# Four of six chunks of a matmul as seven products in every second group, with four-bank evictions and sums by accumulating DMA

## The chip, the cores and the metric

The kernel runs on one core of a Trainium2 chip. Its time is the device time of one execution, in microseconds (us). Before the change it was 1006.78 us, the median of three runs (1006.6 to 1006.91). The profile is of one more execution, with a span of 1005.2 us.

## The reference, cut to what matters

A depthwise causal convolution along the sequence, with seven taps per head and softmax over the taps, then layer norm, then a two-layer block with a residual:

```python
# x: (8, 4224, 192) fp32; weight: (8 heads, 7 taps)
w = softmax(weight, axis=-1)
y[b, s, d] = sum_k w[d // 24, k] * x_pad[b, s + k, d]     # six zeros ahead of each sequence
xn = (y - mean(y)) / sqrt(var(y) + 1e-6) * g_ln           # over d
out = y + relu(xn @ w_ch1) @ w_ch2                        # 192 -> 768 -> 192
```

All is fp32. The weights of the two matmuls come as fp64 and are converted in the kernel; the mean and g_ln are folded into w1, and the division by the standard deviation is applied after the second matmul, as one scale per position (relu allows it).

## The kernel before

Each sequence of 4224 positions is laid out as 128 partitions by 33 rows. The rows are cut into 18 groups: four small ones for the first sequence, then 16 and 17 rows in turn for each of the other seven. While TensorE does group g, VectorE and ScalarE prepare y of group g + 1 and g + 2 (taps), and finish g - 1.

The first matmul ("up", tile ph) makes 768 hidden values in six chunks of 128. A transpose in 32x32 blocks puts 32 channels on partitions, so four matmuls of 32 rows, one for each quarter of the partitions, run side by side; each writes a PSUM bank of its own:

```python
    psum = ctx.enter_context(tc.tile_pool(name="ps", bufs=8, space=PSUM))
    # ... up(g), cut
        for f in range(NF):                               # 6 chunks
            fs = slice(f * P, f * P + P)
            for js in blocks(g):                          # 1 block for 16 rows, 2 for 17
                w = (js.stop - js.start) * C
                ph = [psum.tile([P, 512], F32, tag="ps", ...) for q in range(NQ)]
                for c in range(NC):                       # 6 slices of 32 channels
                    for q in range(NQ):                   # 4 quarters of the partitions
                        rows = slice(C * q, C * q + C)
                        nc.tensor.matmul(
                            ph[q][:, 0:w], w1[rows, c, fs], t[rows, js, c, :],
                            start=(c == 0), stop=(c == NC - 1),
                        )
                for q in range(NQ):
                    # ... dst and src, cut
                    nc.scalar.activation(dst, src, AF.Relu)
            # ... f = 1 to 4: scale and add_to_out of group g - 1, a quarter at a time
```

The second matmul ("down_fast", tile pd) is already done by seven products in place of eight (a Strassen-Winograd scheme: sums of quarters of the hidden values and of w2, seven half-size products, sums of the results). The hidden values are summed in place on VectorE:

```python
    def down_fast(g):
        # ... cs, part, six banks
        def product(bank, left, right, to, first):
            for c in range(CH):
                dst = banks[2 * c + bank]
                # ... matmuls over f and q into dst
                nc.scalar.copy(to[:, c], dst[:, 0:w].rearrange("p (j t) -> p j t", t=T))
        # ... todo: the first and second tap of group g + 2, head by head, on ScalarE
        product(0, a[:, 0, 0], b[0], c11, True)
        some_taps(3)
        product(1, a[:, 1, 0], w2sums[:, 2], c22, True)
        some_taps(3)
        product(1, a[:, 1, 1], w2sums[:, 3], part[:, 1], False)
        some_taps(3)
        product(1, a[:, 0, 1], b[2], part[:, 0], True)
        some_taps(3)
        half_sum(g, (1, 1), (1, 1), (1, 0), ALU.subtract)     # three adds of 1024 each
        half_sum(g, (0, 0), (1, 1), (0, 0), ALU.add)
        half_sum(g, (0, 1), (0, 1), (1, 1), ALU.subtract)
        nc.vector.tensor_tensor(c11, c11, part[:, 0], op=ALU.add)
        product(0, a[:, 1, 1], w2sums[:, 1], c21, False)
        some_taps(2)
        product(0, a[:, 0, 0], w2sums[:, 0], part[:, 2], False)
        some_taps(2)
        product(0, a[:, 0, 1], b[3], c12, False)
```

The second tap of y is added by a DMA that accumulates, from a buffer tb; the other five taps run on VectorE (conv). The loop over groups, for those with seven products:

```python
        up(g)
        conv(g + 1, 2, 5)
        half_sum(g, (1, 0), (0, 0), (1, 0), ALU.subtract)     # the "lower sum"
        conv(g + 1, 5, K)
        transpose(g + 1)
        store_y(g + 1)
        parts = down_fast(g)
        moments(g + 1)                                        # mean and variance per position
        if g % 2 == 0:
            root(g)
        for half in range(last, 2):
            finish_fast(g, half, *parts)                      # add, transpose back
```

Of the kernel before, what the change touches and what calls it, by code (L numbers as in the profile page):

```python
# [16 lines left out]
def kernel(  # L17
# [8 lines left out]
):  # L26

# [17 lines left out]
    nc = tc.nc  # L45
# [33 lines left out]
    T = C // 2  # L79
    CH = NC // 2  # L80
# [11 lines left out]
    spool = ctx.enter_context(tc.tile_pool(name="stat", bufs=3))  # L92
# [4 lines left out]
    psum = ctx.enter_context(tc.tile_pool(name="ps", bufs=8, space=PSUM))  # L97
# [137 lines left out]
    w2sums = consts.tile([P, 4, FC, D // 2], F32, name="w2sums")  # L235
    copy, less, mean = carve(P, F32), carve(P, F32), carve(F, F32)
# [37 lines left out]
    def conv_on_pe(h):  # L274
        n = groups[0][2]
        cs = slice(h * GRP, h * GRP + GRP)
        pc = psum.tile([P, 512], F32, tag="ps", name=f"pc{h}")[:, 0 : n * GRP]
        for k in range(K):
            nc.tensor.matmul(  # L279
                pc, diag[:, h - PE_HEADS[0], k, :], xg[0][:, k : k + n, cs],  # L280
                start=(k == 0), stop=(k == K - 1),
            )
        nc.scalar.copy(y[0][:, 0:n, cs], pc.rearrange("p (j d) -> p j d", d=GRP))

    def centre_w1():
        pm = [psum.tile([P, 512], F32, tag="ps", name=f"pm{r}")[:, 0:FH] for r in range(2)]
        for r in range(2):
            nc.tensor.matmul(pm[r], share[0], w1f[:, r, :], start=True, stop=False)  # L288
        conv_on_pe(PE_HEADS[0])
        for r in range(2):  # L290
            nc.tensor.matmul(pm[r], share[1 + r], w1f[:, 2, :], start=False, stop=True)  # L291
            nc.scalar.copy(mean[:, FH * r : FH * r + FH], pm[r])
        conv_on_pe(PE_HEADS[1])
        first_tap(1, heads=(0, 2))

        for s, parts in (
            (0, [(q, 0) for q in range(NQ)]),
            (2, [(NQ, 0), (NQ + 1, 0), (NQ, 1), (NQ + 1, 1)]),
            (1, [(q, 1) for q in range(NQ)]),
        ):  # L300
            pw = [psum.tile([P, 512], F32, tag="ps", name=f"pw{s}_{q}") for q in range(NQ)]
            for q in range(NQ):
                rows = slice(C * q, C * q + C)
                nc.tensor.matmul(  # L304
                    pw[q][:, 0:FH], copy[rows], w1f[rows, s, :], start=True, stop=False
                )
            for q, (c, r) in enumerate(parts):
                rows = slice(C * q, C * q + C)
                nc.tensor.matmul(  # L309
                    pw[q][:, 0:FH], less[rows], mean[rows, FH * r : FH * r + FH],  # L310
                    start=False, stop=True,
                )
            for q, (c, r) in enumerate(parts):
                nc.scalar.copy(w1[:, c, FH * r : FH * r + FH], pw[q][:, 0:FH])
            if s == 0:
                conv_on_pe(PE_HEADS[2])
                first_tap(1, heads=(2, 4))

    def keep_warm(times):

        idle = psum.tile([P, 512], F32, tag="ps", name="idle")
        for _ in range(times):
            nc.tensor.matmul(idle[:, 0:P], less, copy, start=True, stop=True)
# [66 lines left out]
    def moments(g):  # L390

        n = groups[g][2]
        if g % 2:
            sums[g] = sums[g - 1][:, groups[g - 1][2] :]
        else:
            sums[g] = spool.tile([P, 2 * J, nc.vector.BN_STATS_DIM], F32, tag="st", name=f"st{g}")
        for j in range(n):
            nc.vector.bn_stats(out=sums[g][:, j, :], in_=y[g][:, j, :])  # L398
# [53 lines left out]
    def up(g):  # L452


        n = groups[g][2]
        scaled = {0: (), 1: (), 2: (0, 1)}.get(g, (g - 1,))
        t = yt[g]
# [4 lines left out]
        if fast[g]:  # L462
            halves = room[:, 0:cut].rearrange(
                "p (h e f q j t) -> p h e f q j t", h=2, e=2, f=FC, q=NQ, t=T
# [5 lines left out]
        ht[g] = halves, rest  # L470
        for f in range(NF):
            fs = slice(f * P, f * P + P)
            for js in blocks(g):
                w = (js.stop - js.start) * C
                ph = [
                    psum.tile([P, 512], F32, tag="ps", name=f"ph{g}_{f}_{js.start}_{q}")
                    for q in range(NQ)
                ]
                for c in range(NC):
                    for q in range(NQ):  # L480
                        rows = slice(C * q, C * q + C)
                        nc.tensor.matmul(  # L482
                            ph[q][:, 0:w], w1[rows, c, fs], t[rows, js, c, :],
                            start=(c == 0), stop=(c == NC - 1),
                        )
                for q in range(NQ):
                    src = ph[q][:, 0:w]
                    if js.stop <= fast[g]:
                        dst = halves[:, :, f // FC, f % FC, q, js].rearrange("p h j t -> p j h t")
                        src = src.rearrange("p (j h t) -> p j h t", h=2, t=T)  # L490
                    else:
                        dst = rest[:, f, q, js.start - fast[g] : js.stop - fast[g]]
                        src = src.rearrange("p (j t) -> p j t", t=C)
                    nc.scalar.activation(dst, src, AF.Relu)  # L494
            if 1 <= f <= 4:
                for s in scaled:
                    m = groups[s][2]
                    scale(s, m * (f - 1) // 4, m * f // 4)
                    if f % 2 == 0:
                        add_to_out(s, m * (f - 2) // 4, m * f // 4)  # L500

    po = {}

    def down(g):
# [8 lines left out]
        for c, js in order:  # L513
            w = (js.stop - js.start) * C
            bank = psum.tile([P, 512], F32, tag="ps", name=f"po{g}_{c}_{js.start}")
# [8 lines left out]

    def w2_sums():
        (b11, b12), (b21, b22) = (
            (w2[:, e * FC : e * FC + FC, 0 : D // 2], w2[:, e * FC : e * FC + FC, D // 2 : D])
            for e in range(2)  # L530
        )

        for dst, a, b in ((0, b12, b11), (1, b22, 0), (2, b22, b12), (3, b21, 1)):
            a, b = (w2sums[:, v] if isinstance(v, int) else v for v in (a, b))
            nc.vector.tensor_tensor(w2sums[:, dst], a, b, op=ALU.subtract)

    def half_sum(g, dst, left, right, op):
        a = ht[g][0]
        for f in range(FC):
# [3 lines left out]

    def down_fast(g):
        n = fast[g]
        w = n * T
        a = ht[g][0]
        cs = cpool.tile([P, NC, NFAST * C], F32, tag="cs", name=f"cs{g}")[:, :, 0 : n * C]
        cs = cs.rearrange("p c (j h t) -> p c j h t", h=2, t=T)
        part = cpool.tile([P, 3, CH, NFAST * T], F32, tag="part", name=f"part{g}")[:, :, :, 0:w]  # L550
        part = part.rearrange("p v c (j t) -> p v c j t", t=T)
        banks = [
            psum.tile([P, 512], F32, tag="ps", name=f"pd{g}_{c}_{i}")
            for c in range(CH) for i in range(2)
        ]

        def product(bank, left, right, to, first):
            for c in range(CH):
                dst = banks[2 * c + bank]
                for f in range(FC):  # L560
# [6 lines left out]
                nc.scalar.copy(  # L567
                    to[:, c], dst[:, 0:w].rearrange("p (j t) -> p j t", t=T)
                )

        b = [w2[:, e * FC : e * FC + FC, d * (D // 2) : (d + 1) * (D // 2)]
             for e in range(2) for d in range(2)]
        c11, c21 = cs[:, 0:CH, :, 0], cs[:, 0:CH, :, 1]
        c12, c22 = cs[:, CH:NC, :, 0], cs[:, CH:NC, :, 1]
# [8 lines left out]
        some_taps(3)  # L583
        product(1, a[:, 1, 0], w2sums[:, 2], c22, True)
        some_taps(3)
        product(1, a[:, 1, 1], w2sums[:, 3], part[:, 1], False)
        some_taps(3)
        product(1, a[:, 0, 1], b[2], part[:, 0], True)
        some_taps(3)
        half_sum(g, (1, 1), (1, 1), (1, 0), ALU.subtract)  # L590
        half_sum(g, (0, 0), (1, 1), (0, 0), ALU.add)
        half_sum(g, (0, 1), (0, 1), (1, 1), ALU.subtract)
        nc.vector.tensor_tensor(c11, c11, part[:, 0], op=ALU.add)
        product(0, a[:, 1, 1], w2sums[:, 1], c21, False)
        if g + 1 == NG:
            finish_fast(g, 0, cs, part)
        some_taps(2)
        product(0, a[:, 0, 0], w2sums[:, 0], part[:, 2], False)
# [3 lines left out]
        return cs, part  # L602

    def finish_fast(g, half, cs, part):
        n = fast[g]
        ot = ots[g] if half else out_tile(g)
        fresh = cs[:, CH * half : CH * half + CH, :, 1]
        nc.vector.tensor_tensor(fresh, fresh, part[:, 1 + half], op=ALU.add)  # L608
        for c in range(CH * half, CH * half + CH):
            nc.vector.transpose(  # L610
                ot[:, 0:n, C * c : C * c + C], cs[:, c].rearrange("p j h t -> p j (h t)")
            )

    def park(g):

        n = groups[g][2]
        room = 3 * CH * NFAST * T if g == 0 else NC * NFAST * C
        parked = cpool.tile([P, room], F32, tag="cs" if g else "part", name=f"parked{g}")
# [77 lines left out]
    for g in range(NG):  # L696
        if g + 2 < NG and g not in (3, 4):
            load_x(g + 2)
        up(g)
        last = g + 1 == NG  # L700
        if g == 0:
            first_tap(1, False, heads=(4, H))
        if not fast[g]:
# [14 lines left out]
            if g == 1:  # L718
                finish(0)
                root(0)  # L720
                w2_sums()
# [7 lines left out]
        if not last:  # L729
            conv(g + 1, 2, 5)  # L730
        half_sum(g, (1, 0), (0, 0), (1, 0), ALU.subtract)
        if not last:
            conv(g + 1, 5, K)
            transpose(g + 1)
            if g != 3 and g + 2 < NG:
                store_y(g + 1)
# [6 lines left out]
        if not last:  # L743

            moments(g + 1)
            if g % 2 == 0:
                root(g)
        for half in range(last, 2):
            finish_fast(g, half, *parts)
        if last:  # L750
# [33 lines left out]
```

## Time and profile before

| engine | busy us | share of the span |
|---|---|---|
| PE (TensorE matmul) | 993.9 | 99% |
| PEld (TensorE weight load) | 660.8 | 66% |
| DVE (VectorE) | 844.1 | 84% |
| ACT (ScalarE) | 559.9 | 56% |
| POOL (GpSimd) | 65.7 | 7% |

Of the span, the first matmul has 518.3 us of TensorE, the second 418.9 us (236.9 + 182.0) in groups with seven products and 51.4 us in the others. The clock granted to TensorE is full throughout. A line of the profile names an engine, a line of the kernel, an operation, and the tiles it writes and reads; what follows in square brackets is the idle time ahead of it and what ended it. In the pieces of the chain the columns are start, length, engine, tile and line, and the number of instructions.

### The profile page before, as it was taken

Reading aid. Unit: us, or ns where it says so; the run is one execution under the profiler, and the core shown is the slowest. Engines: PE = TensorE matmul, PEld = TensorE weight load, DVE = VectorE, ACT = ScalarE, POOL = GpSimd, SP = SyncE. Lnnn points to the kernel's source line nnn. Section 1 sums busy time; section 2 is a strip of 40 time slices with the busy share of each in tenths; the row PEclk is TensorE's granted clock in tenths of the full one; section 3 lists DMA queues with packets and bytes.
Section 4 is the critical chain, followed back from the end, with each engine's and each line's share of the span. In section 5 each row is a group of like instructions: output and inputs, shape, how many; then the busy total and the mean of one; then the engine's idle time right before and its main releaser. Section 6 shows DMA issues by size and latency. Waiting matters only on the chain.

```text
span 1005.2 us, 35683 instructions
## 1 busy us (share of the span) xinstructions
PE 993.9 (99%) x16050; PEld 660.8 (66%) x16050; DVE 844.1 (84%) x1552; ACT 559.9 (56%) x1468; POOL 65.7 (7%) x92
## 2 busy tenths in 40 slices
PE   7999999999999999999999999999999999999997
PEld 6888675578545875468654686557854578545786
DVE  7999898898788978979689896889968799788607
ACT  6547464656556564665646566465654656554451
POOL 2001101000000000000000000000001000000000
PEclk9999999999999999999999999999999999999999
DMA  5343717634336363254634535364243734142031
GB/s 193 108 191 55 204 31 219 203 65 110 133 72 194 65 194 88 37 191 84 194 69 83 182 58 182 68 153 137 44 171 75 219 65 106 46 77 37 2 65 69
DMA packets 16102, 114.17 MB, mean 114 GB/s; under 512 B 2127, under 2 KB 2895, under 8 KB 11854
## 3 DMA queue, kind: packets, MB, share of 16 engines
q0 software_dynamic: 9504, 54.17, 27.8%
q1 hardware_dynamic: 6142, 57.73, 14.5%
q8 instruction: 125, 2.05, 0.9%
q14 instruction: 27, 0.22, 0.1%
q10 hardware_dynamic: 304, 0.00, 0.0%
HBM read 38.95 MB, written 50.23 MB: 89 GB/s over the span
## 4 chain that ended last, share of the span: by engine, by line
PE 98%; DVE 1%; DMA 0%; ACT 0%; issue 0%; ACTq 0%
PE ph L482 51%; PE pd L562 40%; PE po L518 5%; PE pc L279 1%; DMA taps<-in_weight_dram 0%; DVE ht L540 0%; PE pw L304 0%; PE pw L309 0%; ACT room L272 0%; DVE y L647 0%; PE pm L288 0%; PE pm L291 0%; DVE room L205 0%; DVE room L197 0%; DVE room L194 0%; ACT room L181 0%
## 5 line engine op out<-in xcount | busy, mean ns | idle before, releaser
L482 PE MATMUL ph<-yt,w 32*128 32x256 f32 (+6 forms) x7200 | 518.3, 443 | 0.1
L482 PEld LDWEIGHTS ph<-yt,w 32*128 32x128 f32 x7200 | 364.3, 185 | 151.0 <-issue 116.3
L373 DVE SCALAR_TENSOR_TENSOR y<-xg,taps,y 128x408 f32<-128x408 f32 (+5 forms) x734 | 365.8, 575 | 33.4 <-issue 33.2
L494 ACT ACTIVATE ht<-ph 128x256 f32<-128x256 f32 (+6 forms) x600 | 222.6, 457 | 228.8 <-PE ph L482 228.1
L540 DVE TENSOR_TENSOR ht<-ht 128x1024 f32<-128x1024 f32 (+2 forms) x180 | 205.4, 1208 | 105.6 <-PE pd L562 74.8
L562 PE MATMUL pd<-ht,w2sums 128*32 128x256 f32 (+2 forms) x4320 | 236.9, 377 | 0.1
L562 PEld LDWEIGHTS pd<-ht,w2sums 128*32 128x32 f32 x4320 | 140.3, 110 | 91.2 <-DVE ht L540 0.5
L562 PE MATMUL pd<-ht,w 128*32 128x256 f32 (+2 forms) x3240 | 182.0, 378 | 0.0
L562 PEld LDWEIGHTS pd<-ht,w 128*32 128x32 f32 x3240 | 103.8, 110 | 73.9 <-issue 8.3
L567 ACT COPY cs<-pd 128x256 f32<-128x256 f32 (+2 forms) x180 | 66.5, 370 | 99.5 <-PE pd L562 99.5
L635 ACT ACTIVATE ot<-ot,r 128x192 f32<-128x192 f32 x247 | 93.1, 471 | 0.0
L567 ACT COPY part<-pd 128x256 f32<-128x256 f32 (+2 forms) x135 | 49.5, 368 | 73.6 <-PE pd L562 73.6
L346 ACT ACTIVATE y<-xg,taps 128x408 f32<-128x408 f32 (+5 forms) x137 | 71.7, 592 | 5.6 <-DVE st L398 5.1
L398 DVE BATCH_NORM_STATS2 st<-y 128x6 f32<-128x192 f32 x264 | 70.2, 342 | 0.0
L359 ACT ACTIVATE tb<-xg,taps 128x384 f32<-128x384 f32 (+1 forms) x112 | 63.4, 619 | 0.0
L639 POOL DMA_DIRECT2D out_dram<-ot x34 | 29.5, 883 | 459.9 <-ACT ot L635 269.3
L610 DVE STREAM_TRANSPOSE ot<-cs 128x512 f32<-128x512 f32 (+2 forms) x90 | 56.6, 679 | 2.5 <-DVE cs L608 0.5
L384 DVE STREAM_TRANSPOSE yt<-y 128x3072 f32<-128x3072 f32 (+5 forms) x19 | 56.2, 2957 | 2.1 <-PE ph L482 0.4
L518 PE MATMUL po<-ht,w 128*32 128x192 f32 (+3 forms) x1152 | 51.4, 339 | 0.0
L362 POOL DMA_DIRECT2D y<-tb x28 | 24.9, 1051 | 351.4 <-ACT cs L567 173.2
L518 PEld LDWEIGHTS po<-ht,w 128*32 128x32 f32 x1152 | 37.1, 110 | 13.7 <-issue 0.8
L608 DVE TENSOR_TENSOR cs<-cs,part 128x768 f32<-128x768 f32 (+2 forms) x30 | 27.7, 925 | 0.0
(79 smaller groups left out, 150.2 us busy)
## 6 DMA issues: line engine op xcount, KB each, us to landing
y<-tb POOLq DMA_DIRECT2D x21, 768.0 KB, 6.4
out_dram<-ot POOLq DMA_DIRECT2D x20, 768.0 KB, 6.8
xg<-in_x_dram SPq DMA_DIRECT2D x6, 2208.0 KB, 13.2
xg<-in_x_dram SPq DMA_DIRECT2D x6, 2112.0 KB, 13.0
out_dram<-y SPq DMA_DIRECT2D x6, 1632.0 KB, 7.8
out_dram<-y SPq DMA_DIRECT2D x6, 1536.0 KB, 8.3
y<-tb POOLq DMA_DIRECT2D x7, 864.0 KB, 10.6
out_dram<-ot POOLq DMA_DIRECT2D x6, 864.0 KB, 7.1
```

What stands on the lines that cost most here:

```text
L346: nc.scalar.mul(dst, src, tap)
L359: nc.scalar.mul(tb[g][:, 0:n, cs], xg[g][:, 1 : 1 + n, cs], taps[:, h, 1:2])
L373: nc.vector.scalar_tensor_tensor(out=y[g][:, 0:n, cs], in0=t[:, k : k + n, cs], scalar=taps[:, h, k : k + 1], in1=y[g][:, 0:n, cs], op0=AL ...
L398: nc.vector.bn_stats(out=sums[g][:, j, :], in_=y[g][:, j, :])
L482: nc.tensor.matmul(ph[q][:, 0:w], w1[rows, c, fs], t[rows, js, c, :], start=(c == 0), stop=(c == NC - 1),)
L494: nc.scalar.activation(dst, src, AF.Relu)
L518: nc.tensor.matmul(bank[C * q : C * q + C, 0:w], w2[:, f, C * c : C * c + C], t[:, f, q, js.start - fast[g] : js.stop - fast[g], :], start ...
L540: nc.vector.tensor_tensor(a[:, *dst, f], a[:, *left, f], a[:, *right, f], op=op)
L562: nc.tensor.matmul(dst[C * q : C * q + C, 0:w], right[:, f, C * c : C * c + C], left[:, f, q], start=(first and f == 0), stop=(f == FC - 1 ...
L567: nc.scalar.copy(to[:, c], dst[:, 0:w].rearrange("p (j t) -> p j t", t=T))
L610: nc.vector.transpose(ot[:, 0:n, C * c : C * c + C], cs[:, c].rearrange("p j h t -> p j (h t)"))
L635: nc.scalar.mul(ots[g][:, j, :], ots[g][:, j, :], rstd[g][:, j : j + 1])
```

## The change

In the six groups 6, 8, ..., 16 (16 rows each) the first matmul takes four of its six chunks in seven products. The rows of positions are halved (8 and 8), the channels are halved (3 and 3 slices), and the four chunks are two and two. Each product is then two chunks wide, 256 columns by 3 slices. The first and the last of the six chunks are done as before and stand ahead of and behind the products. The sums of y are made by VectorE in the buffer tb, the sums of w1 once. Three products accumulate in one set of four banks (the chain) and the running result is copied out between them; what must be added elsewhere is added by DMAs that accumulate in SBUF, and by VectorE for c21. Relu is applied in the last copy, or on SBUF after the sums.

For this PSUM is one tile of eight banks, given out singly or in sets of four; a set is copied out by one instruction in groups with an even number of rows. The order on VectorE and ScalarE is shifted around the products: the moments go ahead of the half sums in part, nine of the scalings go into the second matmul, and one copy in the second matmul (part 0) is left out, VectorE reading the bank instead. The purpose is fewer columns for TensorE, which is busy nearly all the time. The diff, cut:

```diff
+    MIXED = range(6, NG, 2)
+    PAIR = NF // 2 - 1
+    HJ = (J - 1) // 2
+    EARLY = 6
-    psum = ctx.enter_context(tc.tile_pool(name="ps", bufs=8, space=PSUM))
+    psum = ctx.enter_context(tc.tile_pool(name="ps", bufs=1, space=PSUM))
+    all_banks = psum.tile([P, 8, 512], F32, tag="ps", name="ps")
+    turn = [0]
+    def take_bank():
+        i = turn[0] % 8
+        turn[0] = i + 1
+        return all_banks[:, i]
+    def take_set():
+        i = (turn[0] + 3) // 4 * 4 % 8
+        turn[0] = i + 4
+        return all_banks[:, i : i + 4]
...
+    def sums_of_y(g):
+        room = bpool.tile([P, J * D], F32, tag="tb", name=f"ysums{g}")
...
+        nc.vector.tensor_tensor(s1, a21, a22, op=ALU.add)
+        nc.vector.tensor_tensor(s2, s1, a11, op=ALU.subtract)
+        nc.vector.tensor_tensor(s3, a21, a11, op=ALU.subtract)
+        nc.vector.tensor_tensor(s4, a12, s2, op=ALU.subtract)
+    def up_mixed(g):
...
+        banks = plain(PAIR)
+        scale(g - 1, 0, 4)
+        evict_up(g, PAIR, whole, banks)
+        conv(g + 1, 2, 6)
+        chain, other = take_set(), take_set()
+        rows_of_tiles(chain, a11, b11, True, False)
+        evict(chain, c11)
+        scale(g - 1, 4, 5)
+        rows_of_tiles(other, a12, b21)
+        evict(other, late[0])
+        add_by_dma(c11, late[0])
+        rows_of_tiles(chain, s2, w1sums[:, 1], False, False)
+        evict(chain, c21)
+        scale(g - 1, 5, 6)
+        rows_of_tiles(other, s3, w1sums[:, 2], True, False)
+        evict(other, c22)
+        scale(g - 1, 6, 7)
+        rows_of_tiles(chain, s1, w1sums[:, 0], False, False)
+        for i in range(PAIR):
+            one = slice(i, i + 1)
+            evict(chain, late[1 + i], i=one)
+            add_by_dma(c22[:, one], late[1 + i])
+        rows_of_tiles(other, a22, w1sums[:, 3], False)
+        evict(other, late[0])
+        scale(g - 1, 7, 8)
+        add_to_out(g - 1, 0, 8)
+        # c21 += late[0], two adds on VectorE (cut)
+        rows_of_tiles(chain, s4, b22, False)
+        evict(chain, c12, True)
+        nc.scalar.activation(c11, c11, AF.Relu)
+        lower_sum(g, (PAIR,))
+        lower_sum(g, range(PAIR))
+        conv(g + 1, 6, K)
+        banks = plain(PAIR + FC)
+        evict_up(g, PAIR + FC, whole, banks)
+        nc.scalar.activation(c22, c22, AF.Relu)
...
         product(0, a[:, 0, 0], b[0], c11, True)
-        some_taps(3)
+        if g in MIXED:
+            m = groups[g - 1][2]
+            scale(g - 1, 8, m)
+            add_to_out(g - 1, 8, m)
+            some_taps(1)
+        else:
+            some_taps(3)
...
-        product(1, a[:, 0, 1], b[2], part[:, 0], True)
+        product(1, a[:, 0, 1], b[2], None, True)
         some_taps(3)
-        half_sum(g, (1, 1), (1, 1), (1, 0), ALU.subtract)
+        if g in MIXED:
+            transpose(g + 1)
+            moments(g + 1, 0, EARLY)
+        elif g + 1 in MIXED:
+            moments(g + 1)
+            if g + 1 == MIXED[0]:
+                sums_of_quarters(w1sums, *quarters_of_w1())
+        half_sum(g, (1, 1), (1, 1), (1, 0), ALU.add)
...
-        nc.vector.tensor_tensor(c11, c11, part[:, 0], op=ALU.add)
+        # c11 += banks[2c + 1], read in PSUM by VectorE, three adds (cut)
...
         for half in range(last, 2):
             finish_fast(g, half, *parts)
+        if g + 1 in MIXED:
+            sums_of_y(g + 1)
+        if mixed:
+            moments(g + 1, EARLY)
+            root(g)
```

`plain(f)` takes a set and does one chunk as before; `evict` is one ScalarE instruction over the four banks.

## The prediction

> **What bounds the kernel now.** I read the chain that ended last first, for its engine shares, then its pieces in order of time.
>
> ```profile
> PE 98%; DVE 1%; DMA 0%; ACT 0%; issue 0%; ACTq 0%
> ```
>
> ```profile
> 77.80 15.75 PE ph L482 x288
> ...
> 394.97 31.11 PE ph L482 x288
> 426.08 27.33 PE pd L562 x504
> 453.42 33.21 PE ph L482 x576
> 486.63 29.01 PE pd L562 x504
> ```
>
> TensorE is the chain, with no gap between pieces. The line at 394.97 is the first matmul of group 8 (sixteen rows of positions, one of the six groups changed): 288 records, two per fp32 matmul, so 31.11/6 = 5.185 us per chunk of 48 records, 108.0 ns each at 512 columns. The line at 77.80 is group 2, whose matmuls are all 256 wide: 15.75/288 = 54.7 ns. So halving the width costs nearly nothing (2 x 54.7 against 108.0). The second matmul takes 27.33/7 = 3.90 us a product.
>
> Next the table by stage for that group and the following one (columns: busy time and instructions of each engine, clock, DMA share):
>
> ```profile
> 394.97:426.08 31.11, 31.11 (x293) 14.66 (x296) 27.97 (x47) 16.50 (x38) 1.74 (x2) 1.00 0.39 74
> 426.08:453.42 27.34, 27.34 (x509) 16.29 (x508) 22.01 (x37) 16.90 (x40) 1.78 (x2) 1.00 0.58 186
> ```
>
> VectorE is busy 28.0 + 22.0 of 58.4 us: 8.5 us spare, and the new design needs some of it. Where the spare lies is in VectorE's timeline:
>
> ```profile
> 397.62 2.00 DVE L610 STREAM_TRANSPOSE ot<-cs 128x544 f32<-128x544 f32 x3
> 402.65 13.39 DVE L373 SCALAR_TENSOR_TENSOR y<-xg,taps,y 128x408 f32<-128x408 f32 x24 [3.03 <-issue]
> 415.96 3.49 DVE L540 TENSOR_TENSOR ht<-ht 128x1024 f32<-128x1024 f32 x3
> 419.37 8.95 DVE L373 SCALAR_TENSOR_TENSOR y<-xg,taps,y 128x408 f32<-128x408 f32 x16
> 428.42 3.58 DVE L384 STREAM_TRANSPOSE yt<-y 128x3264 f32<-128x3264 f32 x1
> 437.15 10.30 DVE L540 TENSOR_TENSOR ht<-ht 128x1024 f32<-128x1024 f32 x9 [5.15 <-PE pd L562]
> ```
>
> The 3.03 us ahead of the taps is labelled "issue", but the accumulating DMA of the second tap was issued at 392.65 to 394.4, so I read it as that DMA landing. In the six even groups the taps start 9.2, 7.7, 8.9, 9.2, 7.9 and 9.4 us after TensorE enters the group: mean 8.7. The 5.15 us is the only other slack. ScalarE's evictions:
>
> ```profile
> 426.10 2.06 ACT L494 ACTIVATE ht<-ph 128x512 f32<-128x512 f32 x4 [1.38 <-PE ph L482]
> ```
>
> Four banks take 2.06 us; one takes 602 ns at 512 columns, 389 at 256: 0.83 ns a column and 176 ns fixed. One instruction over four banks is then 176 + 2048 x 0.832 = 1.88 us (estimate).
>
> [...] 768 KB landing in 6.4 to 6.8 us and 288 KB in 4.6. That slope puts 1 MB at about 8 us (estimate).
>
> **Part by part, for one changed group, from t = 0 where TensorE enters it.**
>
> Removed: four chunks, 4 x 5.185 = 20.74 us. Added: seven products of 48 records at 256 columns, 7 x 2.625 = 18.38. Gain 2.36 us, times six groups 14.2 us. This is the ceiling, 1.4%.
>
> Bank order: plain chunk to set A, 0 to 5.19; products alternate B (the chain, which keeps accumulating) and A: 7.81, 10.44, 13.06, 15.69, 18.31, 20.94, 23.56. Each set is evicted 1.88 us after its product, plus one 0.34 us scaling instruction, inside the next product's 2.625 us: no stall. But the seventh product is on B, and the last plain chunk is given B too: the set was taken from a counter whose last two takes were B, then A, and nothing is taken for products three to seven. It can't start until the seventh result has been copied out by one four-bank instruction: 23.56 + 1.88 + signalling = 25.55. Stall 2.0 us, in every changed group: 12.0 us. The first matmul then ends at 30.7.
>
> Sums over y: VectorE needs the room of the second tap's buffer, free at 8.7. Two adds of 768 (0.93 each) give s2 at 10.6; it is wanted at 10.44. Stall about 0.2 on average. All four sums end at 12.4.
>
> VectorE after that: 32 taps x 0.558 = 17.9, to 30.3; two adds for c21, 2.3, to 32.6; three lower sums of 1.16, the needed ones at 35.0 and 36.1. The second product of the second matmul wants them at 30.9 + 3.9 = 34.8 and 0.43 later: stall up to 0.8. Then 8 taps (4.5), transpose (3.6), six moments (1.6): 45.8; half sums at 46.9, 48.1, 49.2. The fifth product wants them from about 47.3 to 48.2: stall up to 0.9. Both are at the edge and change sign with 1 us.
>
> ScalarE at that seam: the eviction of the last chunk 1.8, the relu over c22 1.8, nine scalings 3.1, a tap 0.5 stand ahead of the copy that frees bank 1 for the third product. That copy ends near 8.4 after the seam; the bank is wanted at 7.8. Stall 0.6, which overlaps the VectorE stall just before it, so I don't add both.
>
> DMA sums: c11's is issued at 12.4 and lands near 20.4; its source is rewritten at 20.94. It holds with 0.5 us to spare, and any delay beyond about 1 us would lengthen the 2.0 us stall. The other two land long before their relu.
>
> One-instruction evictions and fewer copies save ScalarE time (about 0.2 us per chunk) but ScalarE isn't on the chain: nothing. Moments move into idle time of odd groups (7.6 us before half sums at group 7, 4.3 needed): nothing. Other groups: nothing.
>
> Sum per group: -2.36 + 2.0 + (0.1 for s2 + 0 to 1.7 at the seam, say 1.0) = +0.75; six groups +4.5 us. 1006.8 + 4.5 = 1011.
>
> **Rivals.** First, no stall but the gain: if the last plain chunk did not have to wait, or the wait were hidden, 1006.8 - 14.2 = 993, short of 2%. For it: TensorE waits nowhere now, and the scalings are spaced among the products so that each eviction fits. Against: the set's turn is fixed and one instruction releases all four banks. Second, VectorE becomes the bound: about 6 us of added adds in a pair of groups of 121 us, of which it is busy 103, is no bound on average, but the chain from the landing DMA to the half sums has no slack left. If the DMA lands 2 us later, s2, the lower sums and the half sums each push TensorE: 2 us more per group, 1023. Third, the summing DMA collides with loads and stores and lands after 22: each us late is 6 us in all; 3 us late gives 1025 or more.
>
> **Range and chances.** Sure terms: -14.2 and +12. Soft terms: 0 to 1.8 us per group, or 0 to 11 us, mostly one-sided. That gives 1004.6 to 1015; with half a stall hidden or a DMA late, 1001 to 1022. Two per cent faster (under 986.6) lies below the ceiling of the gain, so it needs something I don't see: 0.02. Two per cent slower (over 1026.9) needs 3.3 us per group of stall beyond what I sum, 0.06. Within: 0.92.
>
> **What would show it.** In the changed profile: matmuls of the products at 54 to 55 ns each; a wait of TensorE for ScalarE of about 2 us six times, at the last plain chunk; smaller waits for VectorE at s2, at the second and fifth products. The first matmul of a changed group should take 30.7 us (31.1 before), its second 28 to 29 (27.3). If the first takes 28.8, the stall is wrong; if the products cost over 58 ns, the gain is. If groups not changed grow, VectorE's lag carries over, which I put at nothing.

## The result, and the profile after

The changed kernel takes 1024.74 us (median of four runs, 1024.21 to 1025.7) against 1006.69 before: a ratio of 1.018, with a 95% interval of 1.0163 to 1.0198. It is slower by 18 us. The range of the prediction ended at 1022.

The chain of work, which before was TensorE without a gap for 98% of the span, is cut in the changed kernel: it can be followed back only to 920 us, and other engines stand in it. The second line is the busy row of the page:

```profile
PE 7%; DVE 2%; issue 0%; DVEq 0%
PE 992.4 (97%) x16914; PEld 710.1 (69%) x16914; DVE 884.6 (87%) x1622; ACT 586.9 (57%) x1243; POOL 81.5 (8%) x110
```

TensorE is busy about as long as before (993.9), though it has less to do: in part because busy time includes matmuls at a lower clock (four chunks of 7.1 us in place of 5.4, below). Its waits, from the view of who waited for whom (total, number, longest; one more, at the start of the kernel, was there before):

```profile
PE ps L520 <- ACT ht L596: 12.6, 6, 2.7
...
PE ps L722 <- ACT cs L728: 2.7, 5, 0.6
PE ps L520 <- DVE ysums L571: 2.4, 3, 0.8
PE ps L520 <- ACT ht L508: 1.4, 1, 1.4
```

The first is the wait at the last plain chunk, five times 2 us, as predicted, and once 2.7. The last stands in group 5, in no changed group. TensorE's timeline of group 8, which answers to the pieces at 394.97 and 426.08 before:

```profile
400.59 10.61 PE L520 MATMUL ps<-yt,w 32*128 32x512 f32 x144
411.07 8.05 PE L520 MATMUL ps<-ysums,w1sums 32*128 32x256 f32 x144
418.91 2.80 PE L520 MATMUL ps<-yt,w1sums 32*128 32x256 f32 x48
421.50 2.80 PE L520 MATMUL ps<-ysums,w 32*128 32x256 f32 x48
426.29 7.13 PE L520 MATMUL ps<-yt,w 32*128 32x512 f32 x48 [1.99 <-ACT ht L596]
433.34 4.09 PE L722 MATMUL ps<-ht,w 128*32 128x256 f32 x72
437.25 4.07 PE L722 MATMUL ps<-ht,w2sums 128*32 128x256 f32 x72
441.88 4.09 PE L722 MATMUL ps<-ht,w2sums 128*32 128x256 f32 x72 [0.56 <-ACT cs L728]
```

The first line holds a plain chunk and two products (10.48 us to the next start), the next three the other five. Products cost what was expected. The fifth line is the find: the last chunk has the same 48 records as any chunk, but its line is 7.13 us long. In groups 14 and 16, after the same wait, it is 5.43:

```profile
796.84 5.43 PE L520 MATMUL ps<-yt,w 32*128 32x512 f32 x48 [1.99 <-ACT ht L596]
```

The table by stage has the granted clock in the column after the busy times, as a mean over the stretch: 0.81 with the slow chunk of group 8, 1.00 in group 14.

```profile
424.30:433.34 9.04, 7.05 (x48) 3.03 (x48) 9.04 (x14) 3.68 (x2) 0.87 (x1) 0.81 0.84 152
794.00:802.30 8.30, 6.31 (x68) 2.91 (x67) 8.30 (x15) 4.26 (x4) 0.87 (x1) 1.00 1.02 182
```

VectorE's timeline of group 8 shows the chain that the prediction walked through:

```profile
408.97 0.96 DVE L570 TENSOR_TENSOR ysums<-yt 128x768 f32<-128x768 f32 x1 [7.08 <-DMA y<-tb]
409.96 0.96 DVE L571 TENSOR_TENSOR ysums<-ysums,yt 128x768 f32<-128x768 f32 x1
...
412.57 17.82 DVE L394 SCALAR_TENSOR_TENSOR y<-xg,taps,y 128x408 f32<-128x408 f32 x32
430.31 2.35 DVE L639 TENSOR_TENSOR ht<-ht,parts 128x1024 f32<-128x1024 f32 x2
432.58 3.49 DVE L696 SCALAR_TENSOR_TENSOR ht<-ht 128x1024 f32<-128x1024 f32 x3
```

It waits 7.1 us for the room of the second tap, until 8.4 after TensorE enters the group, and its last lower sum is done at 436.0, 35.5 after that entry (36.1 predicted).

From the starts of the two matmuls in each timeline, the stages that differ (us; before, each changed group has 31.11 + 27.34):

| group | 5, first | 6 | 8 | 10 | 12 | 14 | 16 |
|---|---|---|---|---|---|---|---|
| before | 33.21 | 31.11 + 27.34 | same | same | same | same | same |
| after, first | 35.66 | 33.69 | 32.75 | 32.62 | 33.26 | 32.00 | 32.00 |
| after, second | 29.01 | 28.10 | 28.10 | 28.11 | 28.11 | 28.46 | 28.46 |

The changed groups cost 15.0 us more than before and group 5 costs 2.45 more. Together 17.4 us, against 17.3 between the spans. From group 4 on all other stages are the same to 0.1 us; the small groups ahead of it differ by some tenths either way.

### The profile page after: what moved, and what is told of

It is laid out like the page before. It is cut to its first block, busy times and chain, and to the rows that moved or that the text cites. A ratio compares the mean times of both kernels' runs of the same rounds, so it can differ in the third digit from the quotient of the medians.

```text
span 1022.5 us, 37346 instructions
## 1 busy us (share of the span) xinstructions
PE 992.4 (97%) x16914; PEld 710.1 (69%) x16914; DVE 884.6 (87%) x1622; ACT 586.9 (57%) x1243; POOL 81.5 (8%) x110
## 5 line engine op out<-in xcount | busy, mean ns | idle before, releaser
L520 PE MATMUL ps<-yt,w 32*128 32x256 f32 (+6 forms) x6624 | 435.2, 417 | 14.0 <-ACT ht L596 12.6
L520 PEld LDWEIGHTS ps<-yt,w 32*128 32x128 f32 x6624 | 337.2, 186 | 109.1 <-issue 56.4
L722 PE MATMUL ps<-ht,w2sums 128*32 128x256 f32 (+2 forms) x4320 | 238.7, 378 | 3.3 <-ACT cs L728 2.7
L687 DVE TENSOR_TENSOR ht<-ht 128x1088 f32<-128x1088 f32 (+2 forms) x162 | 184.4, 1208 | 35.6 <-ACT part L728 24.5
L722 PEld LDWEIGHTS ps<-ht,w2sums 128*32 128x32 f32 x4320 | 139.3, 110 | 97.3 <-ACT cs L728 5.5
L722 PE MATMUL ps<-ht,w 128*32 128x256 f32 (+2 forms) x3240 | 182.0, 378 | 0.0
L722 PEld LDWEIGHTS ps<-ht,w 128*32 128x32 f32 x3240 | 103.8, 110 | 73.9 <-issue 8.3
L508 ACT ACTIVATE ht<-ps 128x256 f32<-128x256 f32 (+2 forms) x312 | 100.8, 410 | 92.6 <-PE ps L520 86.4
L728 ACT COPY cs<-ps 128x256 f32<-128x256 f32 (+2 forms) x180 | 64.0, 371 | 119.2 <-PE ps L722 119.2
L510 ACT ACTIVATE ht<-ps 128x2048 f32<-128x2048 f32 (+5 forms) x48 | 63.3, 1318 | 97.7 <-PE ps L520 97.7
```

What stands on the lines that cost most here:

```text
L508: nc.scalar.activation(dst[:, q], src[:, q], AF.Relu)
L520: nc.tensor.matmul(banks[:, q, i * w : i * w + w], right[rows, c, P * i : P * i + P], left[rows, :, c, :], start=(first and c == 0 and i = ...
L687: nc.vector.tensor_tensor(a[:, *dst, f], a[:, *left, f], a[:, *right, f], op=op)
L722: nc.tensor.matmul(dst[C * q : C * q + C, 0:w], right[:, f, C * c : C * c + C], left[:, f, q], start=(first and f == 0), stop=(f == FC - 1 ...
```

## The experiments

The chips of these runs had the kernel before at about 1009 us, so ratios are compared, and stages in the traces.

**The last chunk in the free set.** Theory one: the wait and the slow clock behind it are the loss. Rival: VectorE stands right behind.

```diff
+        turn[0] += 4          # the set that is free, not the chain's
         banks = plain(PAIR + FC)
```

> The last plain chunk of a changed group is given the set of banks that is free (A), not the chain's (B). If the wait for the seventh product's copy and the slow chunk behind it are the loss, both vanish: 6 x 2.0 us of wait and 4 x 1.75 us of slow clock, 19 us, so 1006 us. If VectorE stands right behind (lower sums ready 2.4 us after the second product of the second matmul wants them), 1012 to 1020 us and a wait of TensorE for line 696. If the loss is elsewhere, it stays near 1024.

The ratio is 1.0131 (1.0114 to 1.0148). The trace is of one more execution:

> The kernel with the last chunk in the free set once more, for its trace, since its profiled execution was disturbed. It gained only about 5 us on the changed kernel, so 14 us less than the wait and the slow clock made out: I expect no wait at the last chunk in any of the six groups, and in its place waits of TensorE for VectorE of 2 to 3 us a group at the second product of the second matmul (lower sums), or of the tracks behind it.

TensorE's timeline of group 6 (the last chunk, then the second matmul):

```profile
303.66 5.36 PE L520 MATMUL ps<-yt,w 32*128 32x512 f32 x48
308.95 4.09 PE L723 MATMUL ps<-ht,w 128*32 128x256 f32 x72
314.57 0.64 PE L723 MATMUL ps<-ht,w2sums 128*32 128x256 f32 x8 [1.52 <-DVE ht L697]
315.70 7.55 PE L723 MATMUL ps<-ht,w2sums 128*32 128x256 f32 x136 [0.50 <-DVE ht L697]
```

The wait at the chunk is gone, and TensorE waits 2.0 us for the lower sums one product later. The first matmul falls to 28.6 to 29.8 us, the second grows to 30.7 to 31.5. So both the theory and the rival hold in part: the wait at the chunk is real, and the same time stands behind it on VectorE. In groups 10, 12 and 14 the clock falls behind these waits too (the 136 matmuls of the last line take 9.2 us there, 7.55 in group 6), so the free set alone doesn't keep it full.

**The wait filled with matmuls.** This tells an idle gap from a mere wait.

```diff
+        rows_of_tiles(other, a22[:, :, 0:2], b22[:, 0:2])    # result never read
         banks = plain(PAIR + FC)
```

> Sixteen matmuls of 256 columns into the free set, their result never read, fill the 2 us in which TensorE waits for the seventh product's copy; the wait itself stays. If the last chunk is slow (7.1 us against 5.4) because the idle gap lowers the clock, it takes 5.2 to 5.4 in all six groups and the time falls by 4 x 1.75 = 7 us to 1017.5. If it is slow for another reason (the summing DMAs, 84% DMA share in that stretch), it stays at 7.1 and the time at 1024.7.

```profile
303.33 1.93 PE L520 MATMUL ps<-yt,w 32*128 32x256 f32 x32
305.52 5.43 PE L520 MATMUL ps<-yt,w 32*128 32x512 f32 x48 [0.26 <-ACT ht L596]
```

The last chunk takes 5.43 us in all six groups, with a granted clock of 1.00 and a DMA share of 1.01 and 0.98 around it in groups 6 and 8 (0.81 and 0.84 in group 8 of the changed kernel, where it was slow), so the idle time and not the DMAs lowered the clock. But the time fell only to a ratio of 1.016 (1.0145 to 1.0175), 2 to 3 us, not 7; the interval overlaps that of the changed kernel, and in the traces the changed groups are 2.9 us shorter together. The stages say why: s2 now comes late in all six groups (first matmul 31.94 to 32.05 in each, where a group with neither costs 30.9), and the second matmul is 28.46 in each, not 28.10. I read this as a slow chunk giving VectorE 1.7 us in which to catch up; no run tests that reading.

**The rest of the change, without products.**

```diff
-    MIXED = range(6, NG, 2)
+    MIXED = range(0)
-        if not last and not mixed and g + 1 not in MIXED:   # moments and root ...
         for half in range(last, 2):
             finish_fast(g, half, *parts)
+        if not last and not mixed and g + 1 not in MIXED:   # ... behind the last sums
```

> No group takes the seven products in the first matmul; the rest of the change stays (four banks copied by one instruction, one copy less in the second matmul, orders on VectorE), and the moments stand behind the last sums in every group, so that the hidden room comes free in time. If only the products' order costs, this is as before: 1006.7 within 1. If the rest of the change costs something in itself, more, up to 1010.

The ratio is 0.9999 (0.999 to 1.0007). Four banks copied by one instruction, the missing copy, and banks handed out by hand cost and gain nothing. Group 5 is back at 33.22 us, from 35.66.

**The gap by itself.** The same kernel, with the last chunk of each group of 16 rows in the set just used:

```diff
             for js in blocks(g):
+                if fast[g] == J - 1 and f == NF - 1:
+                    turn[0] += 4
                 banks = take_set()
```

> As the run without products, but in the seven groups of 16 rows the last chunk is given the set of banks just used, so that TensorE waits for one four-bank copy. A gap by itself: 7 x 2.0 = 14 us more than that run if a wait costs its length; 7 x (2.0 + 1.2) = 22 us more if it also lowers the clock in two cases of three, as in the changed kernel, with last chunks of 7 us in the trace.

The ratio is 1.0179 (1.0164 to 1.0194), 18 us for seven waits. Six of the seven groups have 33.4 us for the first matmul, 2.28 more than 31.11, and the one at 552 us has 35.1. Two of the waits, and the clock over them:

```profile
429.30 5.43 PE L520 MATMUL ps<-yt,w 32*128 32x512 f32 x48 [2.00 <-ACT ht L510]
552.25 7.13 PE L520 MATMUL ps<-yt,w 32*128 32x512 f32 x48 [2.00 <-ACT ht L510]
```

```profile
427.30:434.70 7.40, 5.40 (x53) 2.40 (x53) 7.40 (x14) 3.60 (x6) 0.87 (x1) 1.00 0.31 42
550.20:559.40 9.20, 7.20 (x56) 3.10 (x56) 9.03 (x17) 3.60 (x6) 0.87 (x1) 0.81 0.45 75
```

A wait of 2.0 us thus costs 2.28 (the matmuls on its two sides no longer overlap: 0.18 and 0.10 us, read from the best kernel below), and now and then 1.7 more. Only one in seven was slow here, not two in three: I expected 22 us if the clock fell as often as in the changed kernel, and 14 if not.

**The rooms exchanged.** The sums of y go into the room that is free early, the copies into the second tap's buffer:

```diff
-        room = bpool.tile([P, J * D], F32, tag="tb", name=f"ysums{g}")
+        room = cpool.tile([P, NC * NFAST * C], F32, tag="cs", name=f"ysums{g}")
...
-        room = cpool.tile([P, NC * NFAST * C], F32, tag="cs", name=f"parts{g}")
+        room = bpool.tile([P, J * D], F32, tag="tb", name=f"parts{g}")
```

> The sums of y take the room that the copies had (free as soon as VectorE has finished the group before), and the copies take the second tap's buffer; the wait at the last chunk stays. If VectorE's wait for the second tap's DMA is what delays its chain, s2 no longer stalls and VectorE is up to 4 us earlier at the seam: 0.4 + 0.7 us a group less, 6 us in all, ratio about 1.012. If that wait isn't on the path, 1.018.

The ratio is 1.0157 (1.0138 to 1.0176): less than expected. The waits for s2 are gone in every group (30.92 us for the first matmul of two groups, which is 28.64 + 2.28), but four of six last chunks were slow (groups 8, 10, 12 and 16), and group 5's too (37.33 us). The second matmul stays at 28.1 in five groups, where the 0.56 us wait for ScalarE is left.

**Both.**

> Both at once: last chunk in the free set, rooms exchanged. If the two limits stand one behind the other (each alone gives little), the first matmul of a changed group takes 28.8 us and the second 27.9, 1.5 us less than before a group, so about 998 us, ratio 0.991. If the effects only add, 1.018 - 0.005 - 0.006 = 1.007. If a third wait (P3 for ScalarE, the summing DMA) grows into the room, 1.000.

The ratio is 0.9944 (0.9929 to 0.996), faster than before. Alone the two took 0.005 and 0.002 off the ratio, the second within the noise; together 0.024. By stages, the changed groups became 3.9 and 4.9 us shorter alone and 23.3 together. The limits stand one behind the other. The first matmul takes 28.64 us in five of six groups. The second still has 28.1 to 28.7 against the 27.9 expected, and group 5 its 35.66, which is why it is 0.9944 and not 0.991.

**Scalings and moments moved.** Three of the nine scalings ahead of the second product and six behind it, the taps later, and the moments behind the last sums in group 4:

```diff
-            scale(g - 1, 8, m)
-            add_to_out(g - 1, 8, m)
-            some_taps(1)
+            scale(g - 1, 8, 11)
...
         product(1, a[:, 1, 0], w2sums[:, 2], c22, True)
-        some_taps(3)
+            scale(g - 1, 11, m)
+            add_to_out(g - 1, 8, m)
...     # taps and moments, cut
```

> As the run with both, and besides: the nine scalings in the second matmul split three and six around its second product and the taps moved behind, so that bank 1 is freed before the third product wants it; the moments stand behind the last sums in groups that aren't changed too, so that group 5 doesn't wait for the hidden room. Expected 0.5 us less in each of six groups and 2.3 us less at group 5: 993 us, ratio 0.986. If ScalarE only hands the delay on to the next copy, the same as without it, 0.991.

The ratio is 0.989 (0.9873 to 0.9906). The wait for ScalarE is gone and group 5 is at 33.22 us. In three groups TensorE waits 0.5 us for the half sums instead, and their second matmul stays at 28.2 to 28.3.

**The changed kernel again.**

> The changed kernel once more, unaltered. Stage by stage it should show the same waits (2.0 us at the last chunk in six groups, 0.8 at s2 where it comes, 1.35 at group 5); if the slow clock depends on where the wait falls in a window of its own, the groups in which the last chunk takes 7.1 us are others or of another number than 6, 8, 10 and 12. Ratio 1.016 to 1.018.

The ratio is 1.0176 (1.0157 to 1.0196). The slow last chunks are again in groups 6, 8, 10 and 12, so this run doesn't show that the groups vary; group 5 is slow this time (37.33 us).

The traces show more. In the first trace of the changed kernel the clock falls to 0.50 for 3.41 us behind each of four waits at a last chunk, which costs half of that, 1.7 us, and these falls lie a whole multiple of 3.413 us apart: at 304.20, 427.08, 549.96 and 672.84, each 122.88 = 36 x 3.4133 behind the one before. The time cut into stretches on this grid, first for group 8, where the clock fell, then for group 14, where it did not (the second number is TensorE's busy time):

```profile
423.67:427.08 3.41, 1.42 (x20) 0.74 (x18) 3.41 (x8) 3.08 (x4) 0.87 (x1) 1.00 1.05 196
427.08:430.50 3.42, 3.42 (x20) 1.49 (x16) 3.42 (x7) 0.95 (x1) 0.00 (x0) 0.50 1.04 174
...
792.31:795.72 3.41, 2.55 (x48) 2.14 (x40) 3.41 (x7) 3.03 (x3) 1.36 (x2) 1.00 1.02 192
795.72:799.14 3.42, 2.30 (x24) 1.18 (x28) 3.42 (x7) 2.87 (x2) 0.03 (x1) 1.00 1.08 171
```

In group 8 the whole wait lies in one stretch; in group 14 a boundary cuts it in two. All 25 waits at a last chunk go this way (2.0 to 2.7 us; this kernel twice, the gap by itself, the rooms exchanged): the clock fell behind the 13 that have 1.98 us or more in one stretch, and behind none of the 12 that have 1.91 or less (both ends from the gap by itself, at 552 and 429 us: waits that begin 122.95 us apart, 0.07 more than 36 stretches). In groups 6 to 12 the waits begin 122.9 to 123.1 us apart, nearly 36 stretches, so they meet the boundaries alike. This is read from the traces; no run moved a wait on purpose to test it.

**From group 4 on.** Two kernels with `MIXED = range(4, NG, 2)`, the second also with `EARLY = 2`:

> The version with free set, exchanged rooms and moved scalings, with group 4 (also 16 rows) taking the seven products too. The gain of a group without waits is 31.11 - 28.64 = 2.47 us; if group 4 finds its loads and sums in time, about 2.4 us less than that version, ratio 0.9866. If the other order of loads around groups 3 and 4 keeps VectorE late there, no gain, 0.989.

> Besides, two moments instead of six stand ahead of the half sums. In three of six groups TensorE still waited 0.5 us for the half sums (second matmul 28.2 against 27.34): 1.1 us of moments less ahead of them should remove that, 3 x 0.87 = 2.6 us, ratio 0.984. If the moments behind delay the next group's taps, that shows as a longer odd group and takes it back.

Ratios 1.0038 (1.0024 to 1.0052) and 1.0015 (1.0008 to 1.0022): not the missing gain that the rival gave (0.989), but a loss. Both waits stand at group 4's side, in the first of the two (PE). The ACT and POOL lines show what the second waits for:

```profile
153.85 6.45 PE L723 MATMUL ps<-ht,w2sums 128*32 128x192 f32 x80 [5.35 <-DVE ht L688]
196.45 7.39 PE L520 MATMUL ps<-yt,w 32*128 32x512 f32 x48 [7.14 <-ACT parts L596]
...
194.54 1.87 ACT L596 COPY parts<-ps 128x2048 f32<-128x2048 f32 x1 [8.41 <-DMA ht<-parts]
...
185.56 1.05 POOL L140 MEMSET xg<- 1x1152 f32 x1 [18.05 <-DMA xg<-in_x_dram]
186.56 1.50 POOL L599 DMA_DIRECT2D ht<-parts  x2
```

Group 3 waits 5.35 us for half sums: VectorE now does group 4's moments and the sums of w1 ahead of them, from 145.12 to 152.92. Group 4 waits 7.14 for an eviction, this 8.41 for an accumulating DMA, and that is issued late, since GpSimd waits 18.05 for a load of x to land. So the rival's loads count for group 4; the wait in group 3 comes from an order on VectorE that neither expectation named. From group 6 on, the second kernel has every second matmul at 27.33 or 27.34, so the two moments do their part.

**The best of it.** Groups 6 to 16 as in the change, free set, rooms exchanged, scalings moved, and:

```diff
-    EARLY = 6
+    EARLY = 2
```

> The version with free set, exchanged rooms and moved scalings, groups 6 to 16 as in the change, with two moments instead of six ahead of the half sums. The run that began at group 4 showed every second matmul at 27.33 us with that order, against 28.2 in three of six groups before: 3 x 0.87 = 2.6 us less, ratio 0.9865, about 995.5 us on this chip. If the gain at group 4's side was what made room, the waits stay and the ratio is 0.989.

995.62 us, a ratio of 0.987 (0.9854 to 0.9887): faster than before by 13 us, or 1.3%. Group 8:

```profile
394.64 10.61 PE L520 MATMUL ps<-yt,w 32*128 32x512 f32 x144
405.08 7.95 PE L520 MATMUL ps<-ysums,w1sums 32*128 32x256 f32 x144
412.85 2.77 PE L520 MATMUL ps<-yt,w1sums 32*128 32x256 f32 x48
415.44 2.77 PE L520 MATMUL ps<-ysums,w 32*128 32x256 f32 x48
418.03 5.33 PE L520 MATMUL ps<-yt,w 32*128 32x512 f32 x48
423.29 4.09 PE L723 MATMUL ps<-ht,w 128*32 128x256 f32 x72
```

No wait is left in any changed group but one of 0.52 us in group 12. In the other five the first matmul takes 28.65 us and the second 27.33: 2.47 us less a group, the gain that the prediction put at 2.36.

## Why the prediction was wrong

**The gain** (2.36 us a group): right. It is 31.11 - 28.64 = 2.47 where nothing waits.

**The stall at the last chunk** ("Stall 2.0 us, in every changed group"): its mechanism was right and its length exact (1.99; a four-bank copy takes 1.87 to 1.88 us in the groups by shape, as estimated). Its cost was not. First, the wait costs 2.28: 30.92 against 28.64 in two groups of the run with exchanged rooms. Without it (best kernel, group 8) the last chunk starts at 418.03, 0.18 before the line of the product ahead ends (415.44 + 2.77), and its own line has 5.33 us; behind a wait nothing overlaps, and the line has 5.43. Second, in four groups of six the clock fell behind the gap, and the chunk took 7.11 to 7.13, 1.7 us more. This is the step that failed: "Stall 2.0 us, in every changed group: 12.0 us" charged an idle gap its length, where it cost 2.28 us in two groups and 4.0 in four, before what came back elsewhere. Gaps of 2.0 us and, at group 5 in two traces, 1.35 us were enough for the clock to fall. The filled gap shows that idleness is the cause: the chunk took 5.43 us in all six groups.

**s2** ("Stall about 0.2 on average", of which the sum took 0.1): the place was right, the size was not. It came late in three groups, each 0.8 us of wait and 1.08 us of stage (32.00 against 30.92), so 0.54 on average. The two adds that make it took 0.96 us each in group 8; in the profile before, an add of 768 took 949 ns and one of 1024 took 1217.

**The seam** ("say 1.0"): right in size, in part by luck. The second matmul grew by 0.77 in four groups and 1.12 in two. In the four, 0.56 of it is a wait for ScalarE, as worked out (0.6). But the stall of up to 0.8 for the lower sums, the first part of the term, did not come: the first matmul took 32.0 to 33.7 us and not 30.7, which gave VectorE the time. With the free set it came, at 2.0. The half sums made TensorE wait in group 16 alone (0.49).

**Other groups: nothing.** Wrong for group 5: 2.45 us. One partial sum of group 4's second matmul now lies in the hidden tile, VectorE reads it only after the moments and the root, and ScalarE can't write group 5's hidden values until then. ScalarE's idle 6.2 us ahead of its first eviction names VectorE's sum:

```profile
218.60 2.42 ACT L508 ACTIVATE ht<-ps 128x256 f32<-128x256 f32 x8 [6.19 <-DVE cs L785]
219.04 28.59 PE L520 MATMUL ps<-yt,w 32*128 32x256 f32 x480 [1.35 <-ACT ht L508]
```

With the moments behind the sums it is 33.22 us again. The prediction asked only what the missing copy saves, not who reads the new place of the sum, and when.

**The DMA sums**: right but for one group. A megabyte landed in 7.4 us (median; 8 estimated from accumulating DMAs of 768 and 288 KB), and the 0.5 us of slack ran out in group 12, where it took 9.2 and TensorE's wait was 2.66.

Put together for the trace, with the gain at 2.47: six times (2.28 - 2.47) = -1.1; slow clock 4 x 1.70 = 6.8; s2 3 x 1.08 = 3.2; group 12 0.7; second matmuls 4 x 0.77 + 2 x 1.12 = 5.3; group 5 2.45. The sum is 17.4 us, against 17.3 between the spans. The prediction's 4.5 lacked the clock (6.8), group 5 (2.45), four fifths of s2 (2.6), the lost overlap at the wait (1.7) and group 12 (0.7); the gain and the seam were 0.7 each better than in its sum. This says where the time of the trace stands, not what each mend is worth: with the clock full in all six groups (the filled gap) the ratio was still 1.016. The range treated the stall as a sure term with a fixed cost, so the upper end was too low. The prediction also has a slip: 2% slower is 2.6 us a group above its sum ((1026.9 - 1011.3) / 6), not 3.3, so the 0.06 for it was small. The rivals named the lateness of VectorE, and the run with the free set shows that it stood right behind; but they did not name the clock.

Why the clock falls behind one gap and not behind another of the same length goes with the place of the gap on the grid. Over four traces the gap at the last chunk was followed by a slow chunk in 4, 4 and 4 of 6 cases, but in 1 of 7 where no products were done, and the grid separates all 25. What stays open is the rule behind it: in group 5 a gap of 1.35 us, shorter than all of these, had the clock fall in two traces of six, and with the free set two gaps of 1.8 us together (1.30 and 0.50) were enough in group 10.

## What to carry to other kernels

A gap in a saturated TensorE was dearer here than its length (2.0 us cost 2.28, and 4.0 where the clock fell), so when a change makes one, ask who holds the next set of banks; here a set given by turn, not by who is free, made six. A second limit right behind the first hides the worth of each mend: two changes that took 0.005 and 0.002 off the ratio alone took 0.024 together, so try mends in pairs before dropping them. When a buffer is given a second use, list its readers and their time, also in the groups that the change doesn't touch.

## What the runs showed of the hardware that was not expected

The granted clock fell, to 0.50 for 3.41 us in each of the four cases of the first trace (0.81 as a mean over 9 us), after idle gaps of 2.0 to 2.7 us of which 1.98 or more lay in one stretch of the grid, with 1.4 to 1.7 us lost in the chunk behind (6.8 to 7.13 us in place of 5.43); after the 12 gaps with 1.91 or less in one stretch it did not fall. It fell after 1.35 us at group 5 in two traces of six (37.33 against 35.66 us). After the 0.8 us waits for s2 the products behind them took the usual 8.05 us. Of the lost clock less than half came back when the gaps were filled: four slow chunks, 6.8 us, were gone, and the time fell by 2 to 3, while waits for VectorE grew.
